# A gated MLP on one core: two of the first chunk's eight x slices are transposed by DMA instead of TensorE

## The chip, the cores and the metric

The kernel runs on one core of a Trainium2 chip. The core has a matrix engine (PE in the profile, TensorE in the text; its weight loads are listed apart as PEld), a vector engine (DVE), a scalar engine (ACT), GpSimd (POOL) and a sync engine (SP), whose work here is to issue DMAs. DMAs are issued by SP (queue q1) and, in the opening, by ACT (queue q10); 16 DMA engines work both queues off. The metric is the device time of one execution in microseconds (us). The kernel before takes 592.88 us, the median of three runs that lie between 592.21 and 593.13 us.

## The reference

The inputs are bf16: x is 2048 x 1024, `w_gate` and `w_up` are 1024 x 3584, `w_down` is 3584 x 1024. The GELU is the tanh approximation.

```python
def reference(x, w_gate, w_up, w_down):
    g = jnp.einsum("bsd,df->bsf", x, w_gate)
    u = jnp.einsum("bsd,df->bsf", x, w_up)
    h = _gelu(g) * u
    return jnp.einsum("bsf,fd->bsd", h, w_down)
```

## The kernel before, in words

**Tiling.** The 2048 rows of x are worked on in two halves of 1024 rows, and a half in two chunks of 512 rows. TensorE contracts over partitions, so the gate and up matmuls need x with its 1024 columns on the partitions. These columns are cut into eight slices of 128 (`ko` = 0 to 7, `NKB` = 8). The tile `xT[c][ko]` holds slice `ko` of chunk `c`, transposed: 128 partitions by 512 rows. The 3584 columns of the gate and up weights are cut into 28 tiles of 128, which are loaded in eight groups of 3, 3, 3, 3, 4, 4, 4 and 4 tiles (`GROUPS`). A group of three tiles is 768 KB for the gate and 768 KB for the up weights. Weights live in rings of three buffers each (`wg_ring`, `wu_ring`).

**One tile.** For one weight tile and one chunk, eight matmuls over `ko` make the gate sums in one PSUM bank and eight more make the up sums in another (`pair`, L140; the matmul is L102). ACT and DVE then form the GELU and the product in five steps (class `Evac`) and write them to `hT`, which stays in SBUF. After all eight groups of a half, `down` (L282, matmul L285) multiplies `hT` by `w_down` and `store` copies each result out of PSUM and writes it to memory.

**Order in the first half.** Group 0 on chunk 0 (`first_group`), group 1 on chunk 0, group 2 on chunk 0; then groups 0, 1 and 2 on chunk 1; then groups 3 to 7 on both chunks; then the down projection. In the second half all groups run on both chunks.

**How x gets transposed.** Chunk 0 of the first half comes by plain loads: `xpart` (L171) puts 512 rows of one or two slices into the tiles `xn` (four of them, two slices each). Then `turn(ko)` (L207) transposes a slice on TensorE: four 128x128 transposes (L214) into a PSUM bank, 6 or 7 by turns, which DVE copies to `xT[0][ko]` (L220; for slice 0 in two halves, L223 and L224). All other chunks come by DMA transposes, `xload` (L95, issue at L97), which write `xT` from memory directly: chunk 1 of the first half right after the opening's loads, the second half's chunks one by one during the first half's down projection (L328 to L330).

**The first group.** `first_group` (L234) has its own loop order, so that work can begin before all of x and of the weights is there. For each slice `ko` it does the gate and up matmuls of all three tiles, six matmuls into six banks, and puts `turn(ko + 1)` between them, after the first pair (for slice 0 after the second):

```python
        for ko in range(NKB):
            for j in range(GROUPS[0]):
                mm1(ps[j][0], wg, j, 0, ko)
                mm1(ps[j][1], wu, j, 0, ko)
                if j == (1 if ko == 0 else 0) and ko + 1 < NKB:
                    turn(ko + 1)
```

**The order of the loads.** The program runs under a manual schedule (L153): every engine does its instructions in the order of the code. The opening's loads are written out one by one (L186 to L200), S for SP and A for ACT. SP's part ends with slices 4 and 5 of group 0's gate and up weights, slices 6 and 7 of both (L199, L200), then the whole of group 1 and of group 2, gate before up (L201 to L203, issued at L88), and then the eight transposes of chunk 1 (L204, L205). ACT's part ends with x slices 4 and 5 (L195) and x slices 6 and 7 (L198). After that SP issues a group's weights when the group that used the ring's buffer is done, and `w_down` between them.

Of the kernel before, what the change touches and what calls it, by code (L numbers as in the profile page):

```python
# [14 lines left out]
def kernel(  # L15
# [12 lines left out]
    P = nc.NUM_PARTITIONS  # L28
    bf16 = mybir.dt.bfloat16
# [8 lines left out]
    NKB = Dm // P  # L38
# [14 lines left out]
    NST = 4  # L53
    WDF = 4
    NWARM = 6
    TPC = SCH // P

    pool = ctx.enter_context(tc.tile_pool(name="sb", bufs=1))
# [11 lines left out]
    st_ring = [pool.tile([P, DMW], bf16, name=f"st{r}") for r in range(NST)]  # L70
    warm = nc.const_aps.tensor(1.0, (P, SCH), bf16)
    ident = pool.tile([P, P], bf16, name="ident")
    xn = [pool.tile([P, TPC, 2 * P], bf16, name=f"xn{q}") for q in range(NKB // 2)]
    banks = [psum.tile([P, 512], f32, name=f"bank{b}") for b in range(8)]

    nbank = 0
# [1 line left out]
    def bank():  # L78
        nonlocal nbank
        b = banks[nbank % 8]  # L80
        nbank += 1
        return b

    def wload(eng, ring, w, g, n, ko=None):
        c0, cw = STARTS[g] * P, GROUPS[g] * P
        t = ring[n % NW]
        if ko is None:
            eng.dma_start(  # L88
                out=t[:, :, :cw],
                in_=w[:, c0 : c0 + cw].rearrange("(ko ki) f -> ki ko f", ki=P),  # L90
            )
        else:
            eng.dma_start(out=t[:, ko, :cw], in_=w[ko * P : (ko + 1) * P, c0 : c0 + cw])

    def xload(half, c, ko):  # L95
        s0 = half * HS + c * SCH
        nc.sync.dma_start_transpose(  # L97
            out=xT[c][ko], in_=x2[s0 : s0 + SCH, ko * P : (ko + 1) * P]
        )

    def mm1(ps, w, j, c, ko):
        nc.tensor.matmul(  # L102
            ps,
            lhsT=w[:, ko, j * P : (j + 1) * P],
            rhs=xT[c][ko],
            start=(ko == 0),
            stop=(ko == NKB - 1),
        )
# [49 lines left out]
    def dummy(b, n=SCH):  # L158
        nc.tensor.matmul(b[:, :n], lhsT=warm[:, :P], rhs=warm[:, :n], start=True, stop=True)  # L159
# [6 lines left out]
    nc.scalar.activation(gated, gate[:, :1], ACT.Square)  # L166
    for _ in range(NWARM):
        dummy(banks[5])

    def xpart(eng, ko, n):  # L170
        eng.dma_start(  # L171
            out=xn[ko // 2][:, :, (ko % 2) * P : (ko % 2 + n) * P],
            in_=x2[0:SCH, ko * P : (ko + n) * P].rearrange("(t p) d -> p t d", p=P),
        )

    def wpart(eng, ring, w, ko, n):
        eng.dma_start(
            out=ring[0][:, ko : ko + n, : GROUPS[0] * P],
            in_=w[ko * P : (ko + n) * P, : GROUPS[0] * P].rearrange("(ko ki) f -> ki ko f", ki=P),
        )  # L180
# [3 lines left out]
    S, A = nc.sync, nc.scalar  # L184
# [10 lines left out]
    xpart(A, 4, 2)  # L195
    wpart(S, *G, 4, 2)
    wpart(S, *U, 4, 2)
    xpart(A, 6, 2)  # L198
    wpart(S, *G, 6, 2)  # L199
    wpart(S, *U, 6, 2)  # L200
    for n in (1, 2):  # L201
        wload(nc.sync, wg_ring, w_gate, n, n)
        wload(nc.sync, wu_ring, w_up, n, n)  # L203
# [3 lines left out]
    def turn(ko):  # L207


        tp = [banks[6 + ko % 2].bitcast(bf16)] * 2  # L210
        if ko == 0:
            tp = [banks[6].bitcast(bf16), banks[7].bitcast(bf16)]
        for t in range(TPC):
            nc.tensor.transpose(  # L214
                tp[t // (TPC // 2)][:, t * P : (t + 1) * P],
                xn[ko // 2][:, t, (ko % 2) * P : (ko % 2 + 1) * P],
                ident,
            )
        if ko:
            nc.vector.tensor_copy(out=xT[0][ko], in_=tp[0][:, :SCH])  # L220
        else:
            h = SCH // 2
            nc.vector.tensor_copy(out=xT[0][ko][:, :h], in_=tp[0][:, :h])  # L223
            nc.vector.tensor_copy(out=xT[0][ko][:, h:], in_=tp[1][:, h:SCH])  # L224
# [9 lines left out]
    def first_group():  # L234
        wg, wu = wg_ring[0], wu_ring[0]
        ps = [(bank(), bank()) for _ in range(GROUPS[0])]
        turn(0)
        dummy(banks[5])
        dummy(banks[5], SCH // 2)
        for ko in range(NKB):  # L240
            for j in range(GROUPS[0]):
                mm1(ps[j][0], wg, j, 0, ko)
                mm1(ps[j][1], wu, j, 0, ko)
                if j == (1 if ko == 0 else 0) and ko + 1 < NKB:
                    turn(ko + 1)
        e = [Evac(ps[j][0], ps[j][1], j, 0) for j in range(GROUPS[0])]
        e[0].square()
        e[1].square()
        e[0].cubic()
        e[0].sigmoid()  # L250
        e[1].cubic()
        e[2].square()
        e[0].gelu()
        e[0].product()
        e[1].sigmoid()
        e[2].cubic()
        e[1].gelu()
        e[1].product()
        e[2].sigmoid()
        e[2].gelu()  # L260
        e[2].product()
# [32 lines left out]
    for half in range(NHALF):  # L294
        base = half * NG
        if half == 0:
            first_group()
            group(1, [0])
            group(2, [0])
            for g in range(NG):  # L300
                group(g, [1] if g < NW else range(HSC))
                i = g - 1
                if 0 <= i < len(wd):
                    for q in range(i, len(wd) if g == NG - 1 else i + 1):
                        nc.sync.dma_start(
                            out=wd[q],
                            in_=w_down[q * WDF * P : (q + 1) * WDF * P, :].rearrange(
                                "(fo fi) d -> fi fo d", fi=P
                            ),
                        )  # L310
                prefetch(g + 3)
        else:
            for g in range(NG):
                group(base + g, range(HSC))
                prefetch(base + g + 3)
        k = 0
        xnext = [(c, ko) for c in range(HSC) for ko in range(NKB)] if half + 1 < NHALF else []
        for ss in range(HS // P):
            for dc in range(NDC):
# [8 lines left out]
                if xnext:  # L328
                    c, ko = xnext.pop(0)
# [31 lines left out]
```

## Time and profile before

| what | value |
|---|---|
| median of three runs | 592.88 us (592.21 to 593.13) |
| the profiled execution | 592.08 us |
| its span, first to last instruction | 590.3 us |
| TensorE (PE) busy | 586.1 us, 99% of the span, 2784 matmuls |
| weight loads (PEld) busy | 269.1 us, 46% |
| DVE busy | 244.9 us, 41% |
| ACT busy | 147.7 us, 25% |
| gate and up matmuls, L102 | 215.3 and 215.1 us |
| down matmuls, L285 | 193.9 us |
| transposes on PE, L214 | 3.3 us in 32 instructions |
| copies of transposed slices on DVE, L220 | 3.0 us in 7 instructions, 425 ns each |
| granted TensorE clock | 1.00 |
| DMA traffic | 45.52 MB, mean 77 GB/s |

The page gives an engine's busy time as the union of its instructions. A matmul's own duration (379 ns in the mean) is longer than the distance between two starts in a row, since matmuls are pipelined, so costs on PE are read from starts or from the chain of waits, not from durations. Lines such as L102 are lines of the kernel's source. SPq and ACTq are the instruction queues of SP and ACT, where a DMA's issue shows as an instruction; its landing is a later event, given as the time from issue to landing.

### The profile page before, as it was taken

How to read it: one execution, taken by the hardware profiler on the slowest of the kernel's cores; microseconds unless marked ns; L12 is line 12 of the kernel's file. 1: busy time of each engine (PE TensorE's matmuls, PEld its weight loads, DVE VectorE, ACT ScalarE, POOL GpSimd, SP SyncE). 2: the span in 40 equal slices, each digit the busy share in tenths (PEclk: the TensorE clock that was granted, in tenths of full speed). 3: DMA queues.
4: the chain of work that ended last, by engine and by line, in shares of the span. 5: the costliest groups of instructions: out<-in, count | busy, mean ns of one | idle time of the engine just before them, and what ended most of it. 6: DMA issues, size and time to landing. Idle time of an engine off the chain costs nothing.

```text
span 590.3 us, 6656 instructions
## 1 busy us (share of the span) xinstructions
PE 586.1 (99%) x2784; PEld 269.1 (46%) x2784; DVE 244.9 (41%) x363; ACT 147.7 (25%) x243; POOL 0.7 (0%) x6
## 2 busy tenths in 40 slices
PE   9999999999999999999999999999999999999997
PEld 4444444444444444444444444444444444444445
DVE  2765656565566400000045666565656552000000
ACT  1433333333333200000023333333333331000000
POOL 0000000000000000000000000000000000000000
PEclk9999999999999999999999999999999999999999
DMA  9906926055050321121103134314000000000000
GB/s 259 204 1 192 322 93 214 19 195 178 1 178 1 107 54 37 45 45 40 51 18 108 30 114 143 96 48 140 3 1 2 1 1 9 28 18 19 27 19 28
DMA packets 57726, 45.52 MB, mean 77 GB/s; under 512 B 15712, under 2 KB 54112, under 8 KB 57696
## 3 DMA queue, kind: packets, MB, share of 16 engines
q1 hardware_dynamic: 55552, 44.05, 24.9%
q10 hardware_dynamic: 2144, 1.05, 0.7%
q8 instruction: 22, 0.36, 0.3%
q14 instruction: 8, 0.07, 0.0%
HBM read 37.75 MB, written 4.19 MB: 71 GB/s over the span
## 4 chain that ended last, share of the span: by engine, by line
PE 99%; DVE 0%; ACT 0%; issue 0%
PE bank L102 66%; PE bank L285 33%; PE bank L159 1%; PE bank L214 0%; DVE xT L220 0%; ACT st L277 0%
## 5 line engine op out<-in xcount | busy, mean ns | idle before, releaser
L102 PE MATMUL bank<-xT,wg 128*128 128x512 bf16 x896 | 215.3, 379 | 0.1
L102 PE MATMUL bank<-xT,wu 128*128 128x512 bf16 x896 | 215.1, 379 | 0.0
L285 PE MATMUL bank<-wd,hT 128*128 128x512 bf16 (+2 forms) x952 | 193.9, 366 | 0.0
L285 PEld LDWEIGHTS <-hT 128*128 128x128 bf16 x952 | 90.9, 98 | 102.9
L102 PEld LDWEIGHTS <-wg 128*128 128x128 bf16 x896 | 87.7, 98 | 105.4 <-issue 0.6
L102 PEld LDWEIGHTS <-wu 128*128 128x128 bf16 x896 | 87.7, 98 | 105.0 <-issue 0.4
L124 ACT ACTIVATE sq<-bank 128x512 f32<-128x512 f32 x112 | 66.7, 596 | 172.4 <-PE bank L102 172.4
L135 DVE TENSOR_TENSOR tt<-sg,bank 128x512 bf16<-128x512 bf16 x112 | 77.0, 687 | 75.9 <-ACT sg L132 75.8
L127 DVE SCALAR_TENSOR_TENSOR wq<-sq,bank 128x512 f32<-128x512 f32 x112 | 76.8, 687 | 62.6 <-ACT sq L124 62.6
L132 ACT ACTIVATE sg<-wq 128x512 bf16<-128x512 f32 x112 | 70.5, 629 | 88.4 <-DVE wq L127 88.4
L279 DVE CAST st<-bank 128x512 bf16<-128x512 f32 (+2 forms) x17 | 11.1, 652 | 178.3 <-PE bank L285 178.3
L138 DVE TENSOR_TENSOR hT<-tt,bank 128x512 bf16<-128x512 bf16 x112 | 76.9, 687 | 12.5 <-DVE tt L135 1.0
L277 ACT CAST st<-bank 128x512 bf16<-128x512 f32 (+1 forms) x17 | 9.6, 567 | 178.1 <-PE bank L285 178.1
L220 DVE COPY xT<-bank 128x512 bf16<-128x512 bf16 x7 | 3.0, 425 | 8.1 <-PE bank L214 8.1
L159 PE MATMUL bank<-const-bfloat16-1.0 128*128 128x512 bf16 (+1 forms) x8 | 3.6, 598 | 0.8 <-PEq L345 0.8
L214 PEld LDWEIGHTS <-xn 128*128 128x128 bf16 x32 | 2.5, 102 | 2.5 <-DMA xn<-in_x_dram 1.5
L214 PE MATMUL bank<-ident,xn 128*128 128x128 bf16 x32 | 3.3, 231 | 0.0
L159 PEld LDWEIGHTS <-const-bfloat16-1.0 128*128 128x128 bf16 x8 | 1.0, 136 | 1.9 <-issue 1.9
L165 ACT ACT_TABLE_LOAD x1 | 1.3, 1283 | 0.7 <-PEq L345 0.7
L223 DVE COPY xT<-bank 128x256 bf16<-128x256 bf16 x1 | 0.3, 292 | 2.6 <-PE bank L214 2.6
L163 DVE MEMSET gate<- 128x256 uint32 x1 | 0.3, 272 | 0.9 <-PEq L345 0.9
masks.py:199 POOL TENSOR_SCALAR_AFFINE_SELECT ident<-ident 128x128 bf16<-128x128 bf16 x1 | 0.3, 293 | 0.1
(7 smaller groups left out, 1.1 us busy)
## 6 DMA issues: line engine op xcount, KB each, us to landing
wg<-in_w_gate_dram SPq DMA_DIRECT2D x8, 1024.0 KB, 5.3
wu<-in_w_up_dram SPq DMA_DIRECT2D x8, 1024.0 KB, 7.1
wd<-in_w_down_dram SPq DMA_DIRECT2D x7, 1024.0 KB, 9.3
wg<-in_w_gate_dram SPq DMA_DIRECT2D x7, 768.0 KB, 4.7
wu<-in_w_up_dram SPq DMA_DIRECT2D x7, 768.0 KB, 6.4
out_dram<-st SPq DMA_DIRECT2D x31, 128.0 KB, 1.7
wu<-in_w_up_dram SPq DMA_DIRECT2D x3, 192.0 KB, 4.6
xn<-in_x_dram ACTq DMA_DIRECT2D x2, 256.0 KB, 4.7
```

The costliest lines, as they stand in the source:

```text
L102: nc.tensor.matmul(ps, lhsT=w[:, ko, j * P : (j + 1) * P], rhs=xT[c][ko], start=(ko == 0), stop=(ko == NKB - 1),)
L124: nc.scalar.activation(self.sq, self.g, ACT.Square, scale=GELU_SQRT_C)
L127: nc.vector.scalar_tensor_tensor(out=self.wq, in0=self.sq, scalar=1.0, in1=self.g, op0=ALU.add, op1=ALU.mult)
L132: nc.scalar.activation(self.sg, self.wq, ACT.Sigmoid, scale=GELU_K)
L135: nc.vector.tensor_tensor(out=self.tt, in0=self.sg, in1=self.g, op=ALU.mult)
L138: nc.vector.tensor_tensor(out=self.dst, in0=self.tt, in1=self.u, op=ALU.mult)
L159: nc.tensor.matmul(b[:, :n], lhsT=warm[:, :P], rhs=warm[:, :n], start=True, stop=True)
L214: nc.tensor.transpose(tp[t // (TPC // 2)][:, t * P : (t + 1) * P], xn[ko // 2][:, t, (ko % 2) * P : (ko % 2 + 1) * P], ident,)
L220: nc.vector.tensor_copy(out=xT[0][ko], in_=tp[0][:, :SCH])
L277: nc.scalar.copy(out=st[:, :cw], in_=ps[:, :cw])
L279: nc.vector.tensor_copy(out=st[:, :cw], in_=ps[:, :cw])
L285: nc.tensor.matmul(ps[:, :cw], lhsT=hT[f][:, ss * P : (ss + 1) * P], rhs=wd[f // WDF][:, f % WDF, c0 : c0 + cw], start=(f == 0), stop=(f = ...
```

## The change

Slices 6 and 7 of chunk 0 no longer come as a plain load with a transpose on TensorE. ACT's load of these two slices is gone, and with it the fourth `xn` tile. Instead SP issues two DMA transposes, one per slice, straight into `xT[0][6]` and `xT[0][7]`. They stand behind group 0's last weights and ahead of group 1's and group 2's weights. In `first_group`, `turn` is called for slices 0 to 5 only (`NTURN` = 6), so eight transposes on TensorE and two copies on DVE are no longer there. The matmuls of slices 6 and 7 read tiles that a DMA has written.

```diff
+    NTURN = 6
...
-    xn = [pool.tile([P, TPC, 2 * P], bf16, name=f"xn{q}") for q in range(NKB // 2)]
+    xn = [pool.tile([P, TPC, 2 * P], bf16, name=f"xn{q}") for q in range(NTURN // 2)]
...
     xpart(A, 4, 2)
     wpart(S, *G, 4, 2)
     wpart(S, *U, 4, 2)
-    xpart(A, 6, 2)
     wpart(S, *G, 6, 2)
     wpart(S, *U, 6, 2)
+    for ko in range(NTURN, NKB):
+        xload(0, 0, ko)
     for n in (1, 2):
         wload(nc.sync, wg_ring, w_gate, n, n)
         wload(nc.sync, wu_ring, w_up, n, n)
...
-                if j == (1 if ko == 0 else 0) and ko + 1 < NKB:
+                if j == (1 if ko == 0 else 0) and ko + 1 < NTURN:
                     turn(ko + 1)
```

## The prediction

> **What bounds the kernel now.** I read the busy times first, then the chain of waits, then the chain in order of time for the opening, then SP's queue and the DMA rows for the same stretch. From the page, busy times and the chain:
>
> ```profile
> PE 586.1 (99%) x2784; PEld 269.1 (46%) x2784; DVE 244.9 (41%) x363; ACT 147.7 (25%) x243; POOL 0.7 (0%) x6
> PE 99%; DVE 0%; ACT 0%; issue 0%
> PE bank L102 66%; PE bank L285 33%; PE bank L159 1%; PE bank L214 0%; DVE xT L220 0%; ACT st L277 0%
> ```
>
> PE is busy from start to end, so time can only be won by giving PE less to do, and lost by making it wait. The chain in order of time (start us, length us, what) shows what the two turns of the last slices cost PE:
>
> ```profile
> 9.95 0.40 PE bank L214 x4
> ...
> 13.16 0.22 PE bank L214 x4
> 13.38 1.29 PE bank L102 x6
> 14.68 0.22 PE bank L214 x4
> 14.90 185.18 PE bank L102 x858
> ```
>
> From 9.95 us on PE never pauses. Each block of four transposes lies on the path with 0.22 us; the wait for x ended before ko 6 came. Only the first 10 us hold waits for data, and the change touches none of them. SP's queue in the opening (start us, length us):
>
> ```profile
> 6.58 0.37 SPq L177 DMA_DIRECT2D wg<-in_w_gate_dram  x1
> 7.35 0.37 SPq L177 DMA_DIRECT2D wu<-in_w_up_dram  x1
> 7.76 0.47 SPq L88 DMA_DIRECT2D wg<-in_w_gate_dram  x1
> 8.28 0.58 SPq L88 DMA_DIRECT2D wu<-in_w_up_dram  x1
> 8.90 3.06 SPq L88 DMA_DIRECT2D wg<-in_w_gate_dram  x1
> 12.00 2.33 SPq L88 DMA_DIRECT2D wu<-in_w_up_dram  x1
> 14.37 14.24 SPq L97 DMA_TRANSPOSE xT<-in_x_dram  x8
> ```
>
> The two new transposes go in ahead of the row at 7.76. The rows at 8.90 and 12.00 are long because too much is outstanding by then: they end at 11.96 and 14.33, about when the loads of 7.35 and 7.76 have landed. The first of the eight transposes took 3.54 us for the same reason, the others 1.26. Landings (us after issue), from the DMA rows of windows around single issues: group 1's gate weights, its up weights, the first transpose and the second:
>
> ```profile
> wg<-in_w_gate_dram SPq DMA_DIRECT2D x1, 768.0 KB, 6.6
> wu<-in_w_up_dram SPq DMA_DIRECT2D x1, 768.0 KB, 8.5
> xT<-in_x_dram SPq DMA_TRANSPOSE x1, 9.2
> xT<-in_x_dram SPq DMA_TRANSPOSE x1, 6.1
> ```
>
> So group 1's weights land at 7.76 + 6.6 = 14.4 and 8.28 + 8.5 = 16.8 us, and PE asks for them at 16.9 and 18.6, by the timeline:
>
> ```profile
> 16.89 1.89 PE L102 MATMUL bank<-xT,wg 128*128 128x512 bf16 x8
> ...
> 18.62 1.89 PE L102 MATMUL bank<-xT,wu 128*128 128x512 bf16 x8
> ```
>
> Last, the stage table, where the weights' tail and the first transposes meet (core, window, PE, PEld, DVE, ACT, POOL, clock, DMA share, GB/s):
>
> ```profile
> 18.00:21.00 3.00, 3.00 (x16) 1.35 (x15) 2.76 (x5) 1.85 (x4) 0.00 (x0) 1.00 1.37 319
> 21.00:22.50 1.50, 1.50 (x8) 0.68 (x7) 1.40 (x3) 0.26 (x1) 0.00 (x0) 1.00 1.46 46
> 22.50:24.00 1.50, 1.50 (x8) 0.69 (x7) 0.99 (x2) 0.48 (x1) 0.00 (x0) 1.00 1.02 204
> ```
>
> The queues are occupied at 21.0 to 22.5, yet move 46 GB/s. In the packet records the transposes' packets wait from 20.8 to 22.8 while one engine still works off 768-byte weight packets; a code load (16 KB, 19.70 to 20.85) had held that engine. A transpose waits for the last of the 16 engines.
>
> **Removed.** Eight transposes with their weight loads: 2 x 0.22 = **-0.44 us** on the path. Two copies to xT (L220, 425 ns each) on DVE, which is idle for 1.09 us before each: nothing, since the chain holds one such copy only, at 5.84. One x load of 256 KB and its issue (about 0.47 us) on ACT, which does nothing until 16.02: nothing on the path, but it frees 256 KB / 327 GB/s = 0.80 us of DMA time.
>
> **Added: two transposes on SP.** In the waits of SP's queue the load at 6.58 waits for the x load of 2.26, and that at 7.35 for the up load of 2.73: DMAs share eight completion semaphores in turn, so an issue waits for the landing of the DMA eight places back. With one DMA less, the up load of slices 6 and 7 moves to about 6.99 and the first transpose stands behind the landing of the 2.73 load (7.34). SP then runs: transpose 6 at 7.40 to 8.65, transpose 7 to 9.95 (1.26 each). Behind them on SP stand all loads of groups 1 and 2 and chunk 1's eight transposes.
>
> *When do they land?* The load ahead of them lands at 7.35 + 4.6 = 11.95 now, 0.80 earlier without the x load: 11.15. The first transpose of before landed 0.5 us after the weights ahead of it (23.6 against 12.00 + 11.1 = 23.1), the next at 24.0 and 24.7, so 0.5 to 0.7 each. That gives 11.7 and 12.2 to 12.5. PE asks for slice 6 at 14.08 - 0.22 = 13.86 and for slice 7 at 15.60 - 0.44 = 15.16. Margins of 2.2 and 2.7 us: cost nothing, under the cover of the matmuls of slices 0 to 5. The upper bound is the 2.0 us stall above: 13.7 and 14.5, just in time. It needs a code load at 10 to 11 us; the first is at 19.70 and, counted in PE instructions, comes later with 16 fewer. I take the low end. Were the cover gone, every us after 13.86 would be paid in full.
>
> *The DMA transposes against the rule.* Four of PE's blocks cost 0.22 us, four of the DMA's 0.5 to 0.7 us, on a resource with room. The Trainium skill, VectorE: DVE Perf Modes, "The three transpose paths", puts a 128x128 block at 390 ns on TensorE and 1309 ns through the DMA, and its "Rules for kernel authors" say to use TensorE where PSUM will do, so it speaks against this change. By that figure, an estimate, eight blocks in a row after 11.15 land at 16.4 and 21.6 us, PE would wait some 6 us, and the time would be near 599. The trace has no such price.
>
> **Moved: groups 1 and 2.** Group 1's gate weights are issued at 9.95 instead of 7.76, the up weights at 10.47. The x load of 0.74 landed at 3.1 but its first packets moved some 1.2 us after issue, so these are ready by 11.7, before the transposes ahead end (12.2): no gap. Their landing moves by the transposes less the x load, (1.0 to 1.3) - 0.8 = +0.2 to +0.5: 14.7 and 17.1. PE asks at 16.45 and 18.18. Margin 1.7 and 1.1 us: nothing. Upper bound, with 2.0 us of stall: 19.1, that is 0.9 late. Group 2's loads land at 19.2 and 23.1, wanted at 26.8 and 28.5; chunk 1's last transpose lands at 30.0, wanted at 37: delays of 2 us vanish there.
>
> **The end.** The last store's issue takes 0.89 us where the others take 0.33, beside a code load from 586.32 to 587.83. With 16 PE instructions fewer that load shifts against the end. Ends: it no longer meets the store (-0.56), or meets its data (+0.5, as it would end 1 us later against it). Nothing says which; I take zero.
>
> **Sum.** -0.44. The profiled execution took 592.08 us (span 590.3 and 1.8 around it), which is 0.8 below the median of the runs: 592.08 - 0.44 = 591.6 there, 592.88 - 0.44 = **592.4** on the median. A measurement of this kernel tells about 0.2% (1.2 us) from no change, so this is "no change".
>
> **Rivals.**
> 1. *SP is held (slower).* If each new transpose holds SP as the first of before did (3.54 us), group 1's gate load is issued at 7.40 + 7.1 = 14.5. The page's medians for loads that are not queued are 4.7 and 6.4 us to landing: 19.2 and 21.4. PE waits 2.8 for the gate and 0.4 for the up weights: +3.2 - 0.44 = +2.8, 595.7. With 3.54 + 1.26 the issue is at 12.2, the up weights land at 19.1 and it is +0.5. The gain is gone when the issue comes after 11.7; 0.2% is lost after 12.9. For it: the 3.54 row. Against: three loads of 768 KB were outstanding then, at 7.40 it is five loads of 192 to 256 KB.
> 2. *Engines out of step:* the 2.0 us stall falls on transpose 6. Slices just in time, up weights 0.9 late: -0.44 + 0.9 = +0.5, 593.4. Against: landings at 11.3 to 12.0 of one load are spread over 0.7 us only, and no code load is near.
> 3. *The end gains too:* -0.44 - 0.56 = -1.0, 591.9.
> 4. *Nothing is won*, because the transposes were covered: the chain of before shows no cover, and PE would have to find a new wait of just 0.44: 592.9.
>
> **How the numbers follow.** Forecast 0.62; rival 1 0.14; rival 2 0.08; rival 3 0.12; rival 4 0.04. Slower by over 0.2%: most of rival 1 and a little of 2, 0.13. Faster by over 0.2%: rival 3 with the scatter of runs (592.21 to 593.13), 0.07. Same: 0.80. Range: rival 3 less some scatter, 591.7, up to rival 2 plus scatter, 593.8; only rival 1's upper part and the tails stay out.
>
> **What would show it.** Right: 2776 matmuls on PE, 24 of them transposes; two transposes on SP at about 7.4 and 8.7, each 1.1 to 1.3 us, landed by 12.5; PE's first matmul of group 1 at about 16.45 with no wait; the chain unbroken after 9.95. Wrong: PE's weight loads for the gate and up matmuls waiting for a DMA at 13.9, 15.2, 16.5 or 18.2 us, or an SP transpose of over 2 us. What would break the forecast most surely is a wait between the transposes and the loads next to them that the trace of before, where they stand last, cannot show.

## The result, and the profile after

The changed kernel takes 591.72 us (median of 19 runs, 590.88 to 592.42) where the kernel before, run beside it, takes 592.64 us (19 runs, 591.67 to 593.99). The ratio is 0.9984 with a 95% interval of 0.9977 to 0.9990: 0.9 us faster, where 0.44 us was forecast and called "no change". It is less than the 0.2% that I had set as the bound, but clear of the scatter. The profiled execution took 591.74 us (span 590.0), against 592.08 (590.3) before.

The chain of waits of the changed kernel, by engine and by line, has DMA waits in it that the chain before did not have:

```profile
PE 96%; DMA 2%; SPq 1%; issue 1%; ACT 0%
PE bank L103 63%; PE bank L287 33%; DMA wu<-in_w_up_dram 1%; DMA xn<-in_x_dram 1%; SPq L98 0%; SPq L178 0%; SPq L89 0%; SPq L172 0%; ACT st L279 0%
```

(The lines have moved by one or two: L103 is the gate and up matmul, L98 the DMA transpose, L287 the down matmul. In this trace about 2% of the matmul records are missing, 2723 of 2776, so PE's small idle rows are read from its weight loads.) The wait in the middle of the opening is that for group 1's up weights. The timeline shows it (start us, length us, what, idle time before it):

```profile
16.74 1.89 PE L103 MATMUL bank<-xT,wg 128*128 128x512 bf16 x8
...
18.90 1.90 PE L103 MATMUL bank<-xT,wu 128*128 128x512 bf16 x8 [0.26 <-DMA wu<-in_w_up_dram]
```

The up matmuls start 2.16 us after the gate matmuls instead of 1.73 as before: 0.43 us lost. SP's queue of the changed kernel in the same stretch:

```profile
7.11 0.37 SPq L178 DMA_DIRECT2D wg<-in_w_gate_dram  x1
7.52 0.47 SPq L178 DMA_DIRECT2D wu<-in_w_up_dram  x1
8.04 2.50 SPq L98 DMA_TRANSPOSE xT<-in_x_dram  x2
10.58 0.58 SPq L89 DMA_DIRECT2D wg<-in_w_gate_dram  x1
11.20 0.58 SPq L89 DMA_DIRECT2D wu<-in_w_up_dram  x1
11.83 1.69 SPq L89 DMA_DIRECT2D wg<-in_w_gate_dram  x1
13.56 2.62 SPq L89 DMA_DIRECT2D wu<-in_w_up_dram  x1
16.23 13.87 SPq L98 DMA_TRANSPOSE xT<-in_x_dram  x8
```

The two transposes hold SP for 2.50 us together, as forecast; group 1's loads are issued at 10.58 and 11.20. They land 5.9 and 7.6 us after issue, by the DMA rows, at 16.4 and 18.8. The stage table of the kernel before (window, PE, PEld, DVE, ACT, POOL, clock, DMA share, GB/s) has a full DMA side between 10 and 13 us:

```profile
10.00:11.00 1.00, 1.00 (x8) 0.57 (x9) 0.42 (x1) 0.00 (x0) 0.00 (x0) 1.00 1.11 317
11.00:12.00 1.00, 1.00 (x9) 0.60 (x8) 0.10 (x1) 0.00 (x0) 0.00 (x0) 1.00 1.10 327
12.00:13.00 1.00, 1.00 (x7) 0.41 (x6) 0.33 (x1) 0.00 (x0) 0.00 (x0) 1.00 1.09 324
```

and the changed kernel has a hole there:

```profile
10.00:11.00 1.00, 0.95 (x8) 0.57 (x8) 0.32 (x1) 0.00 (x0) 0.00 (x0) 1.00 1.67 261
11.00:12.00 1.00, 1.00 (x9) 0.53 (x9) 0.10 (x1) 0.00 (x0) 0.00 (x0) 1.00 1.00 154
12.00:13.00 1.00, 1.00 (x8) 0.49 (x6) 0.42 (x1) 0.00 (x0) 0.00 (x0) 1.00 1.04 37
```

The queues count as busy (shares of 1.0 and more) and move a fraction of the bytes. So the opening lost something that I had not charged. In the three other profiles of the changed kernel, taken later, the hole is there too, but its second part looks different: the DMA share is 0.61 to 0.72 from 12 to 13 us, so the queues are partly idle there. One of them:

```profile
12.00:13.00 1.00, 1.00 (x8) 0.41 (x5) 0.42 (x1) 0.00 (x0) 0.00 (x0) 1.00 0.65 156
```

In the first pair of profiles the gain comes from PE's work and from a place that I had entered with zero, the last 5 us. On the two pages, the DMA queues' rows of PE's code loads (16 KB each; packets, MB) are 22 before:

```profile
q8 instruction: 22, 0.36, 0.3%
```

and 21 after:

```profile
q8 instruction: 21, 0.34, 0.2%
```

The load that is missing is the one at 586.32 us. The last two stores then land 2.5 us after issue before (DMA rows of 586 to 592 us):

```profile
q8 instruction: 1, 0.02, 1.6%
issues: line engine op xcount, KB each, median us to landing
out_dram<-st SPq DMA_DIRECT2D x2, 32.0 KB, 2.5
```

and 1.4 us after issue in the changed kernel, in the same rows without a code load:

```profile
issues: line engine op xcount, KB each, median us to landing
out_dram<-st SPq DMA_DIRECT2D x2, 32.0 KB, 1.4
```

From the start of ACT's last copy to the end of the span it is 3.26 us before and 2.64 after.

### The profile page after: what moved, and what is told of

The parts are those of the page before. It is cut to its first block, busy times and chain, and to the rows that moved or that the text cites. A ratio compares the mean times of both kernels' runs of the same rounds, so it can differ in the third digit from the quotient of the medians.

```text
span 590.0 us, 6586 instructions
## 1 busy us (share of the span) xinstructions
PE 582.8 (99%) x2723; PEld 268.4 (46%) x2776; DVE 244.1 (41%) x361; ACT 147.8 (25%) x243; POOL 0.7 (0%) x6
## 4 chain that ended last, share of the span: by engine, by line
PE 96%; DMA 2%; SPq 1%; issue 1%; ACT 0%
PE bank L103 63%; PE bank L287 33%; DMA wu<-in_w_up_dram 1%; DMA xn<-in_x_dram 1%; SPq L98 0%; SPq L178 0%; SPq L89 0%; SPq L172 0%; ACT st L279 0%
## 5 line engine op out<-in xcount | busy, mean ns | idle before, releaser
L103 PE MATMUL bank<-xT,wu 128*128 128x512 bf16 x877 | 213.1, 379 | 1.7 <-DMA wu<-in_w_up_dram 0.8
L103 PE MATMUL bank<-xT,wg 128*128 128x512 bf16 x879 | 213.5, 379 | 1.0
L287 PE MATMUL bank<-wd,hT 128*128 128x512 bf16 (+2 forms) x935 | 193.0, 366 | 0.9
L287 PEld LDWEIGHTS <-hT 128*128 128x128 bf16 x952 | 90.9, 98 | 102.9
L103 PEld LDWEIGHTS <-wu 128*128 128x128 bf16 x896 | 87.5, 98 | 106.7 <-DMA wu<-in_w_up_dram 1.8
L103 PEld LDWEIGHTS <-wg 128*128 128x128 bf16 x896 | 87.7, 98 | 105.3 <-DMA wg<-in_w_gate_dram 0.3
```

The lines of the kernel that those rows point to most:

```text
L103: nc.tensor.matmul(ps, lhsT=w[:, ko, j * P : (j + 1) * P], rhs=xT[c][ko], start=(ko == 0), stop=(ko == NKB - 1),)
L287: nc.tensor.matmul(ps[:, :cw], lhsT=hT[f][:, ss * P : (ss + 1) * P], rhs=wd[f // WDF][:, f % WDF, c0 : c0 + cw], start=(f == 0), stop=(f = ...
```

## Experiments: what the code load at the end and the two transposes are worth

Each time is given against the kernel before, run on the same chip in the same group, with the 95% interval of the ratio.

**The theory, and its rivals.** The theory: PE's 0.45 us, plus a long end that goes with PE's instruction count (5570 before, 5554 after), less what PE now waits for group 1's up weights, because a DMA transpose holds all 16 DMA engines back until the slowest is there. Rivals: the end is shorter for another reason; the lateness comes from SP or from the bytes.

**1. The count put back.** The changed kernel with fourteen warm-up matmuls for six, 5570 instructions.

```diff
-    for _ in range(NWARM):
-        dummy(banks[5])
+    for _ in range(14):
+        dummy(banks[5], 220)
```

> The changed kernel with eight more PE instruction pairs: the six warm-up matmuls of 512 columns become fourteen of 220 columns, the same 3072 columns or so, so PE's program has as many instructions as before (5570). Theory: the change won its time at the end, because a 16 KB code load of PE no longer falls beside the last store. Then the load is back at the end here, the last store's issue takes about 0.9 us instead of 0.33, the stretch from ACT's last copy to the end of the span is 3.3 us instead of 2.7, and the time is about 0.6 us above the changed kernel. Rival: the end is shorter for another reason, such as the stores' position; then the stretch stays at 2.7 us.

591.73 us, ratio 0.9988 (0.9979 to 0.9997). The end was 2.64 us in its profile and the last store's issue 0.33 us: by this the theory was wrong. But the code load had come back, at 591.3 us, after the end of the span. So the count brings the load back; where it falls is another matter. That is taken up in 5 and 6.

**2. The count moved in the kernel before.** Twenty-four warm-up matmuls of 128 columns for six of 512, 5606 instructions.

```diff
-    for _ in range(NWARM):
-        dummy(banks[5])
+    for _ in range(24):
+        dummy(banks[5], 128)
```

> The kernel before, nothing of the change in it, with its six warm-up matmuls of 512 columns as twenty-four of 128 columns: 36 more PE instructions, so PE's code loads come some 1 us earlier against the end. Theory: the last code load ends before the last store and the stretch from ACT's last copy to the end is 2.7 us as in the changed kernel, the time about 0.6 us below the kernel before (0.1%). Rival: the shorter end needs the change's own parts; then the stretch stays at 3.3 us and the time equals before.

591.89 us, ratio 0.9994 (0.9985 to 1.0003). The load stood at 585.65 us, the end was 2.70 us: as the theory has it, with nothing of the change. The time doesn't tell the forecast 0.1% from none.

**3. PE's work put back, the DMAs of the change kept.** Eight matmuls of 128 columns on constants where the two turns stood; 5570 instructions.

```diff
                 if j == (1 if ko == 0 else 0) and ko + 1 < NTURN:
                     turn(ko + 1)
+                elif j == 0 and NTURN <= ko + 1 < NKB:
+                    for _ in range(TPC):
+                        dummy(banks[6 + (ko + 1) % 2], P)
```

> The changed kernel with PE doing eight 128-column matmuls of constants where the two turns of slices 6 and 7 stood, results unused: PE's work and its instruction count (5570) are as before, the DMA side as after. Theory: 0.44 us of PE time comes back and so does the code load at the end (0.6), less what PE no longer waits for group 1's up weights (0.4 in the one profile): time within 0.3 us of the kernel before, start of group 1 about 0.44 later than in the changed kernel. Rival: the DMA transposes themselves are what costs or wins; then it stays near the changed kernel, 0.9 below before.

592.28 us, ratio 0.9999 (0.9990 to 1.0008): the gain is gone, as the theory says. PE needs 5.43 us from the last common turn (slice 5) to group 1, 5.42 in the kernel before and 4.97 in the changed one, so PE's part is 0.45 us. The times agree: the kernel of 1, timed beside this one, has the same count and the same DMAs without these eight matmuls, and takes 0.55 us less. But the profile has a short end, 2.63 us, and by that alone this kernel should have been faster than before. The difference is outside the span: 592.70 - 589.88 = 2.82 us in that execution, 1.78 in the profiles of before and after. Its code load is at 591.7 us, beyond the last instruction.

**4. Plain loads for the two transposes.** Slices 6 and 7 hold other rows of x.

```diff
     for ko in range(NTURN, NKB):
-        xload(0, 0, ko)
+        nc.sync.dma_start(out=xT[0][ko], in_=x2[0:P, (ko % 2) * SCH : (ko % 2 + 1) * SCH])
```

> The changed kernel with two plain loads of the same 128 KB each (128 rows of 1 KB) in place of the two DMA transposes; slices 6 and 7 then hold other rows of x, so this leaves the transposition out. Theory: the DMA transposes stall all 16 engines until the slowest has caught up (1.1 us and 0.8 us in the changed kernel's packet records), which makes group 1's up weights land at 18.8 instead of 17.1. Without them up weights land at 17.0 to 17.4, PE does not wait, time about 0.4 below the changed kernel. Rival: the lateness comes from SP's issue times (2.5 us for two transposes) or from the bytes: SP's issue gets shorter too here, but the up weights would still land after 18 us if bytes are the cause.

591.41 us, ratio 0.9985 (0.9976 to 0.9994), the same as the change. In its stage table the hole is all but gone:

```profile
10.00:11.00 1.00, 0.95 (x8) 0.53 (x8) 0.37 (x1) 0.00 (x0) 0.00 (x0) 1.00 0.96 277
11.00:12.00 1.00, 1.00 (x9) 0.57 (x8) 0.05 (x1) 0.00 (x0) 0.00 (x0) 1.00 0.95 266
12.00:13.00 1.00, 1.00 (x7) 0.44 (x5) 0.42 (x1) 0.00 (x0) 0.00 (x0) 1.00 1.06 303
```

So the hole goes with the transposes. Yet group 1's up weights landed at 18.15 us, not at 17.0 to 17.4, so my expectation for them was wrong: with plain loads of the same bytes they come as late as with the transposes (18.0 to 18.2 us in the three undisturbed profiles of the changed kernel). The rival that named SP isn't separated by this run, because SP's queue changes with it. The two plain loads hold SP for 0.94 us, not 2.50, and group 1's gate weights are issued at 8.82 us, not at 10.3:

```profile
7.83 0.94 SPq L202 DMA_DIRECT2D xT<-in_x_dram  x2
8.82 0.43 SPq L89 DMA_DIRECT2D wg<-in_w_gate_dram  x1
9.29 0.90 SPq L89 DMA_DIRECT2D wu<-in_w_up_dram  x1
```

The up weights, issued at 9.29, land 8.9 us later:

```profile
wu<-in_w_up_dram SPq DMA_DIRECT2D x1, 768.0 KB, 8.9
```

Each load's landing is recorded 16 times, once per DMA engine: for group 1's gate weights the middle one of the 16 is at 13.6 us here and at 15.3 in a profile of the changed kernel, but the last is at 15.8 here and 15.7 there. Here twelve of the 16 are done by 14.1 us, and four engines come 1.4 to 2.2 us behind the middle, at 15.0 to 15.8. A load has landed only when the slowest engine is done. With the transposes the engines arrive closer together but all of them later, without them most run ahead and four lag. That a transpose makes the engines wait for each other fits its own landings (all 16 within 0.1 to 0.2 us in the undisturbed profiles of the changed kernel), but no run shows it apart from SP's later issue. Why four engines lag was not found.

**5. Both kernels again, and two variants.** The kernel before and the changed one, unchanged, for a second profile:

> The kernel before, unchanged, for a second profile. Theory (the code load beside the last store belongs to this program): the last store's issue takes 0.9 us again, a code load stands at about 586.3 us, and the stretch from ACT's last copy to the end is 3.3 us. Rival, for which the run with 5570 PE instructions and a 2.6 us end speaks: the load falls beside the last store in some executions only; then this profile shows 0.33 us and 2.7 us, and the end explains only a part of the 0.9 us in the mean. The time itself should be that of the kernel before, within 0.1%.

> The changed kernel, unchanged, for a second profile and on the same chip as the others of this group. Time 0.4 to 0.9 us below the kernel before. Stretch at the end 2.6 to 2.7 us. In the opening the two DMA transposes land between 12 and 13.7 us; group 1's up weights land at 18 to 18.9 us while PE asks at 18.2 to 18.8, so the wait for them is between 0 and 0.5 us. If the wait belongs to the change and not to that one execution, it shows again with 0.3 us or more.

Before: 592.50 us, ratio 0.9999 (0.9989 to 1.0008). Its end was 2.69 us this time, the code load at 590.9 us: the rival is right, the load falls beside the last store in some executions only. After: 591.39 us, ratio 0.9987 (0.9978 to 0.9996). No code load after 568 us, the end 2.64 us, and no wait for the up weights. The chain of this execution has no DMA in it, from the last turn to the down projection:

```profile
10.54 1.29 PE bank L103 x6
11.84 0.22 PE bank L216 x4
12.06 187.78 PE bank L103 x870
199.83 96.69 PE bank L287 x448
```

The transposes landed at 11.7 and 12.2 us, the weights at 15.7 and 18.1. The first up matmul starts at 18.37, and the weight load ahead of it, which needs the weights first, at 18.18, less than 0.1 us after they landed (18.14). The margin is almost nothing.

Group 1's up weights in two loads of four slices, so that PE can begin with the first half:

```diff
     wload(nc.sync, wg_ring, w_gate, 1, 1)
-    wload(nc.sync, wu_ring, w_up, 1, 1)
+    whalf(wu_ring, w_up, 1, 0, 4)
+    whalf(wu_ring, w_up, 1, 4, 4)
```

> The changed kernel with group 1's up weights as two loads of four slices each (384 KB) instead of one of 768 KB. PE needs the second half 0.9 us after the first, so a lateness of up to 0.9 us is covered. Theory: in the changed kernel PE waits for the up weights on most executions (0.4 us); then this is 0.3 to 0.4 us faster than the changed kernel. Rival: the wait is rare; then it is within 0.2 us of it.

591.57 us, ratio 0.9991 (0.9982 to 0.9999): not faster than the changed kernel beside it (591.39). This speaks for the rival: the wait is rare.

Half the change, slice 7 alone by DMA transpose:

```diff
-    NTURN = 6
+    NTURN = 7
...
     xpart(A, 4, 2)
+    xpart(A, 6, 1)
```

> Half the change: slice 7 alone by DMA transpose, slice 6 by a 128 KB load and TensorE. Eight PE instructions fewer than before instead of sixteen (5562). If PE's work is what was won, 0.22 of the 0.44 us is won here, and one transpose holds up the loads behind it half as much: time 0.2 to 0.3 us below before. If the code load at the end is what was won, it is all there or not at all: 0.6 us or more below before, or 0.2.

592.15 us, ratio 0.9996 (0.9987 to 1.0005). From the last common turn to group 1 it is 5.19 us, so 0.23 us of PE time for one slice, half of 0.45. The time is too close to before to say more.

**6. The end.** Both kernels with 5578 PE instructions (ten warm-up matmuls of 308 columns, and eighteen of 172), and further profiles of the kernel before:

> The kernel before with ten warm-up matmuls of 308 columns instead of six of 512: 5578 PE instructions instead of 5570, the same columns. Theory: with 5570 the last code load is due just where PE's program ends, so it falls beside the last store in some executions and after the end in others (seen once each); with 5578 it is due before PE's end in all of them. Then the load stands at about 586 us, the last store's issue takes 0.9 us, the end is 3.3 us long, and the time is 0.2 to 0.5 us above the kernel before. Rival: the place of the load doesn't follow the count; then the end stays at 2.7 us in this profile and the time at that of before.

> The changed kernel with eighteen warm-up matmuls of 172 columns: 5578 PE instructions here too. Theory: the load stands beside the last store as in its partner without the change, the end is 3.3 us long, and what is left between the two is PE's 0.45 us alone: this is 0.45 us below its partner and within 0.2 us of the kernel before. Rival: the change wins something more than PE's work and the end, say in the opening; then it is 0.7 us or more below its partner.

> The kernel before, unchanged, a third profile. From the start of group 1's gate matmuls to ACT's last copy 570.14 us, as in its two other profiles. The end is 2.7 us (load after the end) or 3.3 us (load beside the last store). Opening: the last turn that both kernels have starts between 11.4 and 12.7 us, set by the landing of x slice 1.

> The kernel before, unchanged, a fourth profile, with the same expectation: 570.14 us in the middle, 2.7 or 3.3 us at the end. If the load falls beside the last store in about half of the executions, one of the two new profiles should show it.

With 5578 the load came before PE's end in both profiles, at 586.3 and 586.7 us, as expected, but cost little: ends of 2.85 and 2.63 us. The times are 592.01 (0.9996, 0.9987 to 1.0005) and 591.92 (0.9994, 0.9985 to 1.0003); that the pair differs by 0.45 us is neither shown nor excluded. The kernel before had the longest ends of all there, 4.03 and 4.17 us, with 591.9 and 591.4 us of span. In the fourth profile the code load lies in the middle of the last store (DMA rows of 586 to 592 us):

```profile
q8 instruction: 1, 0.02, 1.2%
issues: line engine op xcount, KB each, median us to landing
out_dram<-st SPq DMA_DIRECT2D x2, 32.0 KB, 2.2
```

Then the two kernels of 5570 instructions from 1 and 3, the changed kernel and the kernel before, each profiled once more:

> The changed kernel with 5570 PE instructions, second profile. If the count sets the load at the end, whatever the DMAs do, a code load stands between 586 and 592 us, and with luck beside the last store: the end is then 3.3 to 4.2 us instead of 2.6. If the long end belongs to the DMAs of the kernel before, it is 2.6 us again.

> The changed kernel with eight matmuls of constants in place of the turns, 5570 PE instructions, second profile. As for the other kernel of 5570: a code load between 586 and 592 us, the end 2.6 to 4.2 us.

> The changed kernel, 5554 PE instructions, third profile. No code load after 568 us, the last store's issue 0.33 us and the end 2.6 to 2.7 us, in this and every execution. A long end here would refute that the count decides. From group 1's first gate matmul to ACT's last copy 570.14 us, or 0.1 to 0.5 more where PE waits for group 1's up weights.

> The kernel before, fifth profile: the end 2.7 us if the load comes after it, 3.3 to 4.2 if beside the last store. Three of four so far were long.

and 3 and the change were timed again, side by side:

> The changed kernel with eight matmuls of constants in place of the turns, timed again. If the ends of the kernel before are long in the mean (0.73 us over its five profiles), this kernel, with the same PE work and short ends, is 0.3 to 0.7 us below the kernel before. If the ends count for nothing in the mean, it equals the kernel before again, and what the change wins beyond 0.45 us stays unexplained.

> The changed kernel, timed again beside the other: 0.45 us below it by PE's work, less 0 to 0.4 us where it waits for group 1's up weights, and 0.6 to 1.1 us below the kernel before. End 2.6 us, no code load after 568 us.

3 again equals before: 592.45 us, 1.0001 (0.9992 to 1.0010), against my expectation of 0.3 to 0.7 us less. The change again: 591.44 us, 0.9985 (0.9977 to 0.9994). All profiles together (us; "middle" is from group 1's first gate matmul to ACT's last copy, "end" from there to the end of the span, "outside" the execution's time less its span):

| kernel | PE instructions | group 1 starts | middle | end | outside | last code load at |
|---|---|---|---|---|---|---|
| before, five profiles | 5570 | 16.89, 17.47, 17.71, 17.06, 17.25 | 570.14 in all | 3.26, 2.69, 4.03, 4.17, 2.70 | 1.78 to 1.79 | 586.3, 590.9, 588.9, 588.2, 586.7 |
| after, four profiles | 5554 | 16.74, 16.64, 16.70, 16.62 | 570.58, then 570.14 | 2.63 to 2.64 | 1.78 to 1.81 | none after 569 |
| after, PE's work put back, three | 5570 | 17.10, 17.74, 16.84 | 570.14 in all | 2.63 to 2.64 | 2.82, 1.89, 2.74 | 591.7, 591.5, 591.5 |
| after, the count put back, two | 5570 | 17.47, 17.17 | 570.14 in both | 2.64 | 1.89, 2.04 | 591.3, none recorded |

Every run has its span recorded, so the time outside can be counted over all runs. In the 41 runs of the changed kernel it is 1.74 to 1.85 us, never more; in the 22 runs of the two other kernels with 5554 instructions (4 and the split of 5) likewise. In the 119 runs of the kernel before (those beside the experiments and those of 5) it is over 1.9 us in 43, up to 3.25. In the kernels of 5570 instructions with the change's DMAs it is over 1.9 us in 17 of 33, up to 3.38; with 5562 in 4 of 11; with 5578 and 5606 in 6 of 33, but never over 1.96.

What follows: with about 5570 instructions PE's last code load comes where the program ends. It falls, by execution, beside the last store or after the last instruction. In three of the five profiles of the kernel before it goes with a longer end inside the span (3.3 to 4.2 for 2.7 us), in two with neither; over all runs of the kernels of 5570, some 40% have a longer time outside the span (up to 3.4 for 1.8). With 5554 no such load is recorded, and neither is seen. The count decides whether the load comes and whether the time outside is ever long, whatever the DMAs do. That the count alone lengthens the end inside the span isn't shown: with the change's DMAs the end was 2.6 us in all five profiles. What decides where it falls was not found: in the kernel before it fell ahead of the span's end in four of five profiles, in the kernels of 5570 with the change's DMAs in none of five.

**The account.** Mean over 119 runs of before: 592.39 us, of which 590.42 span and 1.97 outside. Mean over 41 runs of after: 591.58, 589.80 and 1.78. Of the 0.81 us (0.64 to 0.98 with 95%), 0.19 (0.13 to 0.25) is outside the span and 0.62 (0.46 to 0.78) inside: PE's work is 0.45 of these, and 0.17 is left for the longer ends less the waits for the up weights (0.43 us in one of four profiles). That last part is as large as its interval and can't be split further: group 1's start scatters by over 0.5 us from execution to execution in every kernel (the landing of x slice 1 moves its turn between 5.3 and 6.8 us), and this scatter is larger.

The kernel before with nothing but its count moved (2, and the first of the pair with 5578) is 0.33 and 0.25 us below the kernel before beside it in the mean, each less than its own interval (0.36 and 0.26). With PE's 0.45 that would about close the account. Against it stands the changed kernel with 5578, 0.36 us above the mean of the changed kernel's runs, which nothing here explains.

## Why the prediction was right or wrong

- **PE's work, -0.44 us:** right. 0.45 for two slices and 0.23 for one, and the 570.14 us behind it are the same in every profile but the one with the wait, so all of it arrives at the end.
- **The transposes on SP and their landing:** right in size (1.19 and 1.25 us of SP; landing at 11.6 to 11.7 and 12.1 to 12.3 us in three of four profiles). In the first profile, where the opening ran late, it was 13.1 and 13.7. PE waited for them in none. Rival 1, SP held for 3.54 us by a transpose, is refuted. One reading behind it was wrong without harm: of the other seven transposes of before one took 2.82 us, not 1.26 (the third, issued at 19.27). The figure from the Trainium skill, VectorE: DVE Perf Modes, "The three transpose paths" (1309 ns a block; the prediction's estimate from it was 16.4 and 21.6 us for the landing) does not describe this case: the second set of four blocks landed 0.5 us after the first.
- **Group 1's weights, "+0.2 to +0.5" and "no gap":** wrong. They landed at 15.7 and 18.1 us for 14.7 and 17.1 in the undisturbed profiles, so the margin to the first up matmul was 0.2 us, not 1.1, and the weight load ahead of it had 0.1 us or less: that PE waited in only one of four profiles was luck. The step that failed let group 1's packets follow the transposes with no gap and charged bytes alone; the DMA side moved 154 and 37 GB/s between 11 and 13 us instead of 327 and 324. What makes the landing late is open: plain loads of the same bytes close most of the hole and the up weights still land at 18.15 us, when the slowest four engines are done. Rival 2 foresaw such a stall, on transpose 6. It costs PE 0.43 us in one profile, where rival 2 had 0.9, and there the sign that the prediction had named, a weight load waiting at about 18.2 us, appeared.
- **"The end. [...] Nothing says which; I take zero":** the failed step that decides. The term was not zero. With 16 instructions fewer the last code load no longer comes, and with it go the long times outside the span: 0.19 us in the mean, where the sum had only a fixed "1.8 around it". Inside the span another 0.17 us, as large as its interval, may be the end's. Rival 3, to which I gave 0.12, had the place, but neither the size (0.56 us in every execution) nor the part outside. I had the reason for a shift and treated it as a matter of chance, and I took one profile for the kernel: the end is 2.7 to 4.2 us long in others.
- **The sum and the range:** 591.72 us lies at the edge of the range, 591.7 to 593.8, which reached the wrong way. "No change" was wrong by the measurement's own interval, -0.23% to -0.10%; the bound of 0.2% that I stated is wider than this measurement's scatter.

## What to carry to other kernels

When a change alters the number of instructions on an engine, look where that engine's last code load falls: near the program's end it cost up to 1.6 us in single executions here and 0.19 us or more in the mean, and part of it lies outside the span where no row of the profile shows it. Loads behind two DMA transposes landed 1.0 us later than their bytes let expect, but loads behind plain loads of the same bytes did so too: count a load as landed when the slowest of the 16 engines is done, and put nothing down to the transposes before a run without them has been read the same way. In a kernel whose engine is busy from start to end, compare stages from one fixed event to the next: parts that agree to 0.01 us from profile to profile leave only the scattering ones to explain.

## What the runs showed of the hardware that was not expected

- PE's code loads (16 KB, some 27.6 us apart in most of the program) scatter by execution at the program's end, from 586.3 to 590.9 us in five profiles of one program, and the time outside the span, 1.8 us otherwise, rises to 3.4 us in some executions of programs that make one there.
- Without transposes four of the 16 DMA engines landed their parts of a load 1.4 to 2.2 us after the middle one (15.0 to 15.8 against 13.6 us). In the undisturbed profiles of the changed kernel the 16 landings of each of the two transposes were within 0.2 us, and those of the load ahead of them within 0.1 us; with the same transposes and PE's work put back, that load's were 1.0 us apart in one profile.
